# Loading chunks 6 and 7 in blocks and transposing them on VectorE in a fused retention and MLP kernel

## The chip, the cores and the metric

The kernel runs on one core of a Trainium2 chip. The metric is device time in microseconds (us) of one execution; lower is better. Each kernel is run several times, and the median stands for it.

TensorE does the matmuls and writes to PSUM, VectorE and ScalarE do elementwise work and copies out of PSUM, GpSimd does a few small things, and SyncE issues the transfers between memory and the core's SBUF.

## The reference

Two stages follow each other. The first is a retention layer with a decaying state, for 4 batches, 8 heads, 768 positions and a head size of 64. The second is an MLP with a gated activation over the 3072 rows of 512 values that the first gives.

```python
# q, k, v: (B=4, H=8, S=768, D=64), float32
gamma = 1.0 - 2.0 ** (-5.0 - np.arange(H))
state = 0
for t in range(S):
    state = gamma * state + einsum('bhd,bhe->bhde', k[:, :, t], v[:, :, t])
    y[:, :, t] = D ** -0.5 * einsum('bhd,bhde->bhe', q[:, :, t], state)

x = y.transpose(0, 2, 1, 3).reshape(3072, 512)
h = x @ w_in                       # (3072, 512) @ (512, 2048)
sp = softplus(h)
out = (h * erf(sp)) @ w_out        # (3072, 2048) @ (2048, 512)
```

The weights come as float64.

## The kernel before

The positions are cut into 24 chunks of 128 (6 for each batch), and chunk j goes through these steps: `K_` scales k and q by powers of the decay, `T` transposes k and q so that the head dimension lies on the partitions, `S_` multiplies k and q to scores, `M` masks them, `O_` makes the output and the new state, `A` adds to the state.

The MLP works on groups g, each of a quarter of the hidden units. Groups 0 to 3 are the plain groups: they handle the first 512 rows with ordinary matmuls (`hidden`, then the activation `gate`, then the second layer `project` of the group before). From group 4 (G0) on, each group handles 256 rows and computes its matrix products by seven products of half-size matrices with sums formed ahead (`hidden_part(g, p)` and `project_part(g, p)`, p from 1 to 7). During the plain groups VectorE also converts the float64 weights to float32, piece by piece.

Chunks from NB on are loaded differently: k a second time and q in 32x32 blocks, so placed that VectorE's transpose of single blocks gives the whole transposed chunk. Before the change NB is 8.

```python
    JPC = TCH // C                      # 4
    NB = 2 * JPC

    def load_blocks(to, src):
        for s, d in itertools.product(range(2), range(2)):
            part = slice((2 * s + d) * 32, (2 * s + d + 1) * 32)
            for u in range(HP):         # HP = 4
                nc.sync.dma_start(      # 16 transfers of 16 KB
                    to[part, u * C : (u + 1) * C].rearrange("p (a d) -> p a d", d=32),
                    src[2 * u + s, :, d * 32 : (d + 1) * 32].rearrange("(a p) d -> p a d", p=32),
                )

    def load(j):
        # ...
        else:
            KQ[j] = loads.tile([P, 2, H, D], F32, name="kq")      # 3 buffers
            V[j] = loads.tile([P, H, D], F32, name="v")           # 3 buffers
        now = slice(c * C, (c + 1) * C)
        if j >= NB:
            KB[j] = loads.tile([P, HP * C], F32, name="kb", bufs=2)
            nc.sync.dma_start(KQ[j][:, 0], k[b, :, now, :].rearrange("h p d -> p h d"))
            load_blocks(KQ[j][:, 1].rearrange("p h d -> p (h d)"), q[b, :, now, :])
            load_blocks(KB[j], k[b, :, now, :])
        for i, src in enumerate((k, q) if j < NB else ()):
            # ... one transfer of 256 KB each
        # ...
        nc.sync.dma_start(V[j], v[b, :, now, :].rearrange("h p d -> p h d"))

    def ret_scale(j):                                             # K_
        # ...
        if j >= NB:
            nc.vector.tensor_tensor(                              # L390
                KQ[j][:, 0], KQ[j][:, 0],
                kq_s[:, j % NC, 0, :, None].to_broadcast([P, H, D]), op=ALU.mult,
            )
            for i, x in enumerate((KB[j], KQ[j][:, 1].rearrange("p h d -> p (h d)"))):
                # ...
                by = kq_b[:, j % NC, i, :, :, None].to_broadcast([P, HP, 4, 32])
                nc.vector.tensor_tensor(x, x, by, op=ALU.mult)    # L397
            return
        by = kq_s[:, j % NC, :, :, None].to_broadcast([P, 2, H, D])
        nc.vector.tensor_tensor(KQ[j], KQ[j], by, op=ALU.mult)    # L400
        pace(-1.1)

    def ret_transpose(j):                                         # T
        if j >= NB:
            for name, store, x in (("k", KT, KB[j]), ("q", QT, ...)):
                store[j] = ret.tile([P, HP, C], F32, name=name + "T")
                nc.vector.transpose(store[j].rearrange("p u t -> p (u t)"), x)   # L410
            return
        for i, (name, store) in enumerate((("k", KT), ("q", QT))):
            p = ret_psum()
            for u in range(HP):
                nc.tensor.transpose(p[:, u, :], ..., ident)       # L415
            store[j] = ret.tile([P, HP, C], F32, name=name + "T")
            nc.scalar.copy(store[j], p)                           # L421
        pace(1)
```

The plain groups call their steps from a list, `after`, with one entry per `hidden(g, u)`: steps that run at once, and steps that are put into `waiting` and run in the middle of the next `hidden` or `project`. The steps of the second layer of group g - 1 stand at the end of group g.

```python
    for g in range(G0):
        for u in range(FG):
            if g and u == (2 if g == 1 else 0):
                waiting.append((gated, g - 1))
            hidden(g, u)
            run(after[g][u][0])
            waiting.extend(after[g][u][1])
        gate(g)
        if g:
            for tt in range(TT):
                project(g - 1, tt)
                if g == 1 and tt == 1:
                    waiting.append((K_, 5))
```

The first group after them, g = 4, for chunk j = 6:

```python
        hidden_part(g, 1)
        hidden_part(g, 2)
        if first:
            gated(g - 1)
        # ...
        if first:
            T(j)
        hidden_part(g, 6)
        if first:
            S_(j)
            M(j)
            K_(j + 1)
            block_scales()
        for _ in range(2):
            next(last_steps, None)
        # ...
        hidden_part(g, 5)
        if first:
            T(j + 1)
        hidden_part(g, 7)
        # ...
        if first:
            project(g - 1, 0)
        # ...
        hidden_part(g, 4)
        hidden_part(g, 3)
```

In `hidden_part`, products 1, 6, 7 and 4 use one PSUM bank and products 2, 5 and 3 the other. After product 2 VectorE adds its bank to h (L732), and product 5 then begins that bank anew. The products are L719, the plain first layer L648, the plain second layer `project` L662, and `project_part` L791.

Of the kernel before, what the change touches and what calls it, by code (L numbers as in the profile page):

```python
# [45 lines left out]
def kernel(  # L46
# [21 lines left out]
    JPC = TCH // C  # L68
# [15 lines left out]

    KQ, V, KB = {}, {}, {}

    NB = 2 * JPC

    def load_blocks(to, src):

# [4 lines that stand above are left out]
                nc.sync.dma_start(  # L95
# [5 lines that stand above are left out]
        b, c = divmod(j, NC)  # L101
        if j == JPC - 1:

            x = act.tile([P, N], F32, name="e", bufs=1)
            KQ[j] = x[:, : 2 * d_model].rearrange("p (i h d) -> p i h d", i=2, h=H)
            V[j] = x[:, 2 * d_model : 3 * d_model].rearrange("p (h d) -> p h d", h=H)
        else:
            KQ[j] = loads.tile([P, 2, H, D], F32, name="kq")
            V[j] = loads.tile([P, H, D], F32, name="v")
# [8 lines that stand above are left out]
            queue = nc.scalar if i and 0 < j < 3 else nc.sync  # L118
            queue.dma_start(KQ[j][:, i], src[b, :, now, :].rearrange("h p d -> p h d"))  # L119
        if j == JPC - 1:  # L120
            load_piece(0)
        nc.sync.dma_start(V[j], v[b, :, now, :].rearrange("h p d -> p h d"))
# [36 lines left out]
    def load_piece(n):  # L159
        which, i = pieces[n]  # L160
        w = raws[place[n]]
        if which == "in":
            for r in range(2):
                nc.sync.dma_start(
                    w[r * D : (r + 1) * D].rearrange("p (g f) -> p g f", g=n_k),
                    w_in[r * DH : (r + 1) * DH, i * 2 * P : (i + 1) * 2 * P].rearrange(
                        "(g p) f -> p g f", p=D
                    ),
                )
        else:  # L170
            for d in range(2):
                nc.sync.dma_start(
                    w.rearrange("p (d f c) -> p d f c", d=2, f=2)[:, d],
                    w_out[i * 2 * P : (i + 1) * 2 * P, d * DH : (d + 1) * DH].rearrange(
                        "(f p) c -> p f c", p=P
                    ),
                )
# [175 lines left out]
    def block_scales():  # L353
        nc.vector.reciprocal(by_b[:, 0], by_b[:, 1])
        nc.vector.reciprocal(kq_b[:, 0, 1], kq_b[:, 0, 0])
        nc.vector.tensor_scalar(kq_b[:, 0, 1], kq_b[:, 0, 1], unscale, None, op0=ALU.mult)
        for c in range(1, NC):
            nc.gpsimd.tensor_tensor(
                kq_b[:, c], kq_b[:, c - 1], by_b[:, :, :, None].to_broadcast([P, 2, HP, 4]),
                op=ALU.mult,  # L360
            )
# [16 lines left out]
    def ret_psum(pool=None):  # L378

        pool = pool or (next(psum_turn) if early else ps_r)  # L380
        return pool.tile([P, HP, C], F32, name="hp" if pool is ps_h else "r")
# [3 lines left out]
    def ret_scale(j):  # L385
        if j >= NJ:
            return
        scaled.add(j)
        if j >= NB:
            nc.vector.tensor_tensor(  # L390
# [12 lines left out]
    def ret_transpose(j):  # L403
        assert j in scaled
        if j >= NB:
            for name, store, x in (
# [196 lines left out]
    def gate(g):  # L603


        name = "r" if g < 4 and g % 2 else "e"
        E[g] = act.tile([P, N], F32, name=name, bufs=1)
        nc.scalar.activation(E[g], HS[g], AF.Softplus)  # L608

        if g:  # L610
            gate_erf(g)
# [8 lines left out]
    waiting = []  # L620
# [9 lines left out]
    def run(steps):  # L630
        for f, *args in steps:
            f(*args)

    def gated(g):
        for a in range(2):
            half = slice(a * N // 2, (a + 1) * N // 2)
            nc.vector.tensor_tensor(E[g][:, half], HS[g][:, half], E[g][:, half], op=ALU.mult)  # L637
        pace(-2.2)


    def hidden(g, u):
        ft = g * FG + u
        if u == 0:
            HS[g] = act.tile([P, N], F32, name="h")
        need("in", ft)
        p = ps_h.tile([P, TCH], F32, name="hp")
        for kk in range(n_k):
            nc.tensor.matmul(  # L648
                p, w_in_of(ft, kk), XC[0][:, kk, :], start=(kk == 0), stop=(kk == n_k - 1)
            )  # L650
        nc.scalar.copy(HS[g][:, u * TCH : (u + 1) * TCH], p)
        done.add(("hidden", ft))

        pace_around(3.4 if g else 2.5)
# [27 lines left out]
    G0 = n_ft // FG  # L682
# [5 lines left out]
    def chunk_of(g):  # L688
        return TCH // SCH + (g - G0) // 2
# [116 lines left out]
    def put_part(m, step):  # L806
# [27 lines left out]
    K_, T, S_, M, O_, A = (  # L834
        ret_scale, ret_transpose, ret_scores, ret_mask, ret_out, ret_add
    )
# [6 lines left out]
    for j in range(JPC):  # L843
# [8 lines left out]
        else:  # L852
# [19 lines left out]
            ([(S_, 4)], [(M, 4)]),  # L872
        ],
        [
            ([(O_, 4), (load, 6)], [(A, 4)]),
            ([(T, 5), (load, 7)], []),
            ([(S_, 5)], [(M, 5)]),
            ([(O_, 5)], [(A, 5)]),
        ],
        [  # L880
            ([(load_block_scales,)], []),
            ([], [(x_sums, G0)]),
            ([(load, 8)], [(K_, 6)]),
            ([], []),
        ],
    ]
    for g in range(G0):
# [10 lines that stand above are left out]
                project(g - 1, tt)  # L898
                if g == 1 and tt == 1:
                    waiting.append((K_, 5))  # L900

    j = JPC + 2
    put = None
    for g in range(G0, NG):
        first = g == G0
        more = j < NJ
# [4 lines that stand above are left out]
        if put is not None:  # L913
            for step in range(3):
                put_part(put, step)
        if first:
            T(j)
        hidden_part(g, 6)
        if first:
            S_(j)  # L920
            M(j)
            K_(j + 1)
            block_scales()
        for _ in range(2):
            next(last_steps, None)
        if put is not None:
            put_part(put, 3)
            put = None
        if not first:
            g_sums(g - 1)  # L930
        hidden_part(g, 5)
        if first:
            T(j + 1)
        hidden_part(g, 7)
        for _ in range(2):
            next(last_steps, None)
# [3 lines that stand above are left out]
            project_part(g - 1, 1)  # L940
        hidden_part(g, 4)
        hidden_part(g, 3)


        if more and not first:
            sub_visit(j, g)
        elif more:
            O_(j)
            A(j)
            SC[j + 1] = [ret_psum(ps_h) for _ in range(2)]  # L950
            sub_scores(j + 1)
            sub_mask(j + 1)
        if g + 1 < NG and (g - G0) % 2:
            x_sums(g + 1)
        if more:
            if j + 2 < NJ:
                K_(j + 2)
                T(j + 2)
            if j + 3 < NJ:
                load(j + 3)  # L960
            j += 1
        if first:
            gate(g)
            for tt in range(1, TT):
                project(g - 1, tt)
            put_first()
        else:
            for p in (2, 4):
                project_part(g - 1, p)
            gate(g)  # L970
            for p in (5, 6, 7, 3):
                project_part(g - 1, p)
            if (g - G0) % 2 == 0:
                put = chunk_of(g - 1)
        if g == NG - 1:
            last_gated(g)
        else:
            gated(g)

    g, m = NG - 1, chunk_of(NG - 1)  # L980
# [55 lines left out]
```

## Time and profile before

| | |
|---|---|
| median of 3 runs | 689.3 us (689.06 to 690.34) |
| profiled run, span | 688.0 us |
| ScalarE busy | 257.6 us (37%) |
| transfers | 47.12 MB, mean 68 GB/s |
| issues of 16 KB blocks on SyncE | 256 for q and 256 for k, median 1.8 and 1.7 us from issue to landing |
| issues of 256 KB of v | 23, median 3.1 us from issue to landing |

The profile is one execution as the hardware profiler took it. Its page gives the busy time of each engine, the chain of work that ended last (followed back from the last instruction to whatever released it), the groups of instructions by source line, and the transfers. An engine's instructions can also be listed in order of time, with the idle time before them and the instruction that ended it. A line such as L719 is a line of the kernel. PE is TensorE's matmul, PEld its weight load, DVE is VectorE, ACT is ScalarE, POOL is GpSimd, SPq is SyncE's queue of transfers.

### The profile page before, as it was taken

What the parts mean: (1) busy time and instruction counts of PE and PEld (TensorE: products, weight loads), DVE (VectorE), ACT (ScalarE), POOL (GpSimd) and SP (SyncE); (2) the same over time, 40 slices, a digit from 0 to 9 for tenths busy, and PEclk for the clock granted to TensorE, in tenths of its full rate; (3) what the DMA queues carried; (4) which work ended last, traced back from release to release, by engine and by line L of the source; (5) the groups of instructions that cost most, each with busy time, mean ns of one, the idle gap of its engine ahead of it and who ended that gap; (6) DMA issues with size and microseconds to landing.
All of it is one profiled execution on the core that took longest, in us unless ns stands there. A gap on an engine that the chain in (4) does not pass through costs nothing.

```text
span 688.0 us, 14344 instructions
## 1 busy us (share of the span) xinstructions
PE 678.0 (99%) x6214; PEld 577.8 (84%) x6214; DVE 384.0 (56%) x591; ACT 257.6 (37%) x293; POOL 6.6 (1%) x21
## 2 busy tenths in 40 slices
PE   8899999999999999999999999999999999999997
PEld 8544444586999999999999999999999999999996
DVE  4799999264954643653564455454544554343324
ACT  3377362425234144144242342441441432433430
POOL 2000000010000000000000000000000000000000
PEclk9999999999999999999999999999999999999999
DMA  9999963102322321322222222322222200000000
GB/s 193 212 239 243 240 193 62 28 1 44 104 39 40 75 43 35 75 33 46 64 47 44 67 41 46 71 37 44 51 60 41 48 34 1 2 32 1 1 31 32
DMA packets 147216, 47.12 MB, mean 68 GB/s; under 512 B 135760, under 2 KB 136016, under 8 KB 147152
## 3 DMA queue, kind: packets, MB, share of 16 engines
q1 hardware_dynamic: 144640, 45.66, 30.4%
q8 instruction: 49, 0.80, 0.5%
q10 hardware_dynamic: 2512, 0.53, 0.5%
q14 instruction: 15, 0.12, 0.1%
HBM read 39.86 MB, written 6.29 MB: 67 GB/s over the span
## 4 chain that ended last, share of the span: by engine, by line
PE 86%; DVE 8%; issue 2%; SPq 1%; DMA 1%; ACT 0%; DVEq 0%
PE hp L719 36%; PE o L791 36%; PE o L662 6%; PE hp L648 2%; PE r L527 1%; PE hp L492 1%; DVE w_out_sb L215 1%; DVE w_out_sb L220 1%; DMA e<-in_q_dram 1%; SPq L119 1%; DVE w_out_sb L223 1%; PE o L563 1%; DVE w_in_sb L223 1%; DVE w_in_sb L229 1%; PE hp L542 1%
## 5 line engine op out<-in xcount | busy, mean ns | idle before, releaser
L719 PE MATMUL hp<-xs,w_in_sb 128*128 128x128 f32 x1280 | 149.8, 275 | 0.0
L719 PEld LDWEIGHTS hp<-xs,w_in_sb 128*128 128x128 f32 x1280 | 147.8, 192 | 1.6 <-issue 0.5
L791 PE MATMUL o<-w_out_sb,h 128*128 128x256 f32 x640 | 141.7, 379 | 0.0
L791 PEld LDWEIGHTS o<-w_out_sb,h 128*128 128x128 f32 x640 | 121.6, 190 | 16.5
L719 PE MATMUL hp<-xT,w_in_sb 128*128 128x128 f32 x960 | 113.7, 275 | 0.0
L719 PEld LDWEIGHTS hp<-xT,w_in_sb 128*128 128x128 f32 x960 | 111.9, 192 | 1.9 <-issue 1.0
L791 PE MATMUL o<-w_out_sb,e 128*128 128x256 f32 x480 | 112.1, 383 | 0.0
L637 DVE TENSOR_TENSOR e<-h,e 128x1024 f32<-128x1024 f32 x42 | 49.6, 1222 | 102.7 <-ACT e L618 102.7
L791 PEld LDWEIGHTS o<-w_out_sb,e 128*128 128x128 f32 x480 | 88.2, 190 | 11.6
L648 PE MATMUL hp<-xT,w_in_sb 128*128 128x512 f32 x128 | 56.6, 595 | 0.8 <-DVE w_in_sb L229 0.7
L744 DVE TENSOR_TENSOR h<-h,hp 128x512 f32<-128x512 f32 x20 | 13.8, 688 | 75.3 <-PE hp L719 75.3
L608 ACT ACT_TABLE_LOAD x24 | 30.8, 1283 | 61.1 <-issue 45.4
L648 PEld LDWEIGHTS hp<-xT,w_in_sb 128*128 128x128 f32 x128 | 23.8, 190 | 29.8 <-issue 27.3
L618 ACT ACTIVATE e<-e 128x2048 f32<-128x2048 f32 (+1 forms) x23 | 42.1, 1836 | 0.2
L608 ACT ACTIVATE e<-h 128x2048 f32<-128x2048 f32 x22 | 42.0, 1910 | 0.2
L732 DVE TENSOR_TENSOR h<-h,hp 128x512 f32<-128x512 f32 x20 | 13.8, 688 | 49.6 <-PE hp L719 49.6
L742 ACT COPY h<-hp 128x512 f32<-128x512 f32 x20 | 11.7, 586 | 60.2 <-PE hp L719 60.2
L737 ACT COPY h<-hp 128x512 f32<-128x512 f32 x20 | 11.7, 587 | 57.9 <-PE hp L719 57.9
L735 ACT COPY h<-hp 128x512 f32<-128x512 f32 x20 | 11.7, 586 | 55.3 <-PE hp L719 55.3
L618 ACT ACT_TABLE_LOAD x24 | 30.8, 1283 | 0.4
L581 ACT COPY xT<-r 128x256 f32<-128x256 f32 x32 | 10.4, 375 | 54.8 <-PE r L527 54.8
L730 ACT COPY h<-hp 128x512 f32<-128x512 f32 x20 | 11.8, 588 | 48.3 <-PE hp L719 48.3
(134 smaller groups left out, 674.1 us busy)
## 6 DMA issues: line engine op xcount, KB each, us to landing
w_out_sb<-in_moe_w_out_dram SPq DMA_DIRECT2D x14, 512.0 KB, 5.7
w_in_sb<-in_moe_w_in_dram SPq DMA_DIRECT2D x12, 512.0 KB, 12.0
kq<-in_k_dram SPq DMA_DIRECT2D x23, 256.0 KB, 3.5
v<-in_v_dram SPq DMA_DIRECT2D x23, 256.0 KB, 3.1
out_dram<-r SPq DMA_DIRECT2D x23, 256.0 KB, 3.3
kq<-in_q_dram SPq DMA_DIRECT2D x256, 16.0 KB, 1.8
kb<-in_k_dram SPq DMA_DIRECT2D x256, 16.0 KB, 1.7
w_out_sb<-in_moe_w_in_dram SPq DMA_DIRECT2D x4, 512.0 KB, 10.3
```

Source lines behind the costliest of these rows:

```text
L223: nc.vector.scalar_tensor_tensor(power, hi, 1 << 31, power, op0=ALU.bitwise_and, op1=ALU.bitwise_or)
L608: nc.scalar.activation(E[g], HS[g], AF.Softplus)
L618: nc.scalar.activation(E[g][:, half], E[g][:, half], AF.Erf)
L637: nc.vector.tensor_tensor(E[g][:, half], HS[g][:, half], E[g][:, half], op=ALU.mult)
L648: nc.tensor.matmul(p, w_in_of(ft, kk), XC[0][:, kk, :], start=(kk == 0), stop=(kk == n_k - 1))
L662: nc.tensor.matmul(O[0][tt].rearrange("p (d c) -> p d c", d=2), E[g][:, u * TCH + tt * P : u * TCH + (tt + 1) * P], w_out_of(ft), start=(f ...
L719: nc.tensor.matmul(bank[:, u, :], w_in_sb[:, s, IN[a], kk, u * P : (u + 1) * P], XS[m][b][:, kk, :], start=(p in (1, 2, 5) and u == 0 and ...
L730: nc.scalar.copy(h["11"], flat)
L732: nc.vector.tensor_tensor(h["11"], h["11"], flat, op=ALU.add)
L735: nc.scalar.copy(h["12"], flat)
L744: nc.vector.tensor_tensor(h["12"], h["12"], flat, op=ALU.add)
L791: nc.tensor.matmul(O[m][i][:, half, :], G[g][a][:, u * P : (u + 1) * P], w_out_sb[:, s, OUT[b], u, :], start=i not in started, stop=(s == ...
```

## The change

Chunks 6 and 7 are treated as the later chunks are: NB goes from 8 to 6, so k and q of them come in blocks too, and VectorE transposes them, in place of TensorE with copies by ScalarE. For that the scales of the blocks have to be there earlier (`load_block_scales` still stands in group 3, but `block_scales` moves there as well), and the scaling and transposing of both chunks is put among the second-layer steps of group 3, the `project(2, tt)`. Their loads move from group 2 to group 3, after the scales, and the load of chunk 8 goes behind them. The aim is to take 16 transposes out of TensorE's stream and to use time in which VectorE has nothing to do.

```diff
-    NB = 2 * JPC
+    NB = JPC + 2
@@ the steps after hidden(g, u), for g = 2 and 3
         [
-            ([(O_, 4), (load, 6)], [(A, 4)]),
-            ([(T, 5), (load, 7)], []),
+            ([(O_, 4)], [(A, 4)]),
+            ([(T, 5)], []),
             ([(S_, 5)], [(M, 5)]),
             ([(O_, 5)], [(A, 5)]),
         ],
         [
-            ([(load_block_scales,)], []),
+            ([(load_block_scales,), (load, 6)], []),
+            ([(load, 7)], []),
             ([], [(x_sums, G0)]),
-            ([(load, 8)], [(K_, 6)]),
-            ([], []),
+            ([], [(block_scales,)]),
         ],
@@ after project(g - 1, tt)
                 if g == 1 and tt == 1:
                     waiting.append((K_, 5))
+                elif g == G0 - 1 and tt in (0, 2):
+                    waiting.extend([(K_, JPC + 2 + tt // 2), (T, JPC + 2 + tt // 2)])
+                elif g == G0 - 1 and tt == 1:
+                    load(JPC + 4)
@@ in the groups from G0 on
-        if first:
-            T(j)
         hidden_part(g, 6)
         if first:
             S_(j)
             M(j)
-            K_(j + 1)
-            block_scales()
@@
         hidden_part(g, 5)
-        if first:
-            T(j + 1)
         hidden_part(g, 7)
```

## The prediction

> **What bounds the kernel now.** I read the page first: busy times and the shares of the chain that ended last.
>
> ```profile
> PE 678.0 (99%) x6214; PEld 577.8 (84%) x6214; DVE 384.0 (56%) x591; ACT 257.6 (37%) x293; POOL 6.6 (1%) x21
> ...
> PE 86%; DVE 8%; issue 2%; SPq 1%; DMA 1%; ACT 0%; DVEq 0%
> ```
>
> TensorE is busy for 678.0 of 688.0 us, and the chain is its own work for 86%. VectorE's 8% lies before 92 us, where the chain in order of time steps through the weight conversions; after that it is TensorE alone up to the end. So a microsecond taken from TensorE's stream after 92 us counts in full, and a microsecond of waiting put into it counts in full too. The total of VectorE, 56%, tells nothing here: what matters is when one of its instructions is late.
>
> Next, TensorE's instructions in order of time, where the first group after the plain ones begins (columns: start us, us, engine, line, operation, tiles; a matmul is two records).
>
> ```profile
> 138.60 1.04 PE L415 MATMUL r<-ident,kq 128*128 128x128 f32 x8
> 139.47 1.95 PE L719 MATMUL hp<-xs,w_in_sb 128*128 128x128 f32 x16
> 141.35 1.16 PE L428 MATMUL r<-qT,kT 64*128 64x128 f32 x16
> 142.44 2.05 PE L719 MATMUL hp<-xs,w_in_sb 128*128 128x128 f32 x16
> 145.06 1.06 PE L415 MATMUL r<-ident,kq 128*128 128x128 f32 x8 [0.57 <-issue]
> 145.96 1.95 PE L719 MATMUL hp<-xs,w_in_sb 128*128 128x128 f32 x16
> ```
>
> L415 is the transposes of chunks 6 and 7, between the products 2, 6, 5 and 7. The first takes 139.47 - 138.60 = 0.87 us of the stream. The second takes 145.96 - 145.06 = 0.90, and 0.57 us stand idle before it: they end when VectorE has scaled chunk 7 (L400, next but one fence). A product of 16 records takes 1.79 us of the stream (the chain in order of time), so from start to start the second costs 145.96 - 142.44 - 1.79 = 1.73 us.
>
> Then SyncE's issues, as chunk 8 is already loaded in blocks by this kernel (columns as above; the duration is the time the queue spent on them).
>
> ```profile
> 100.86 8.59 SPq L347 DMA_DIRECT2D kq_b<-decay_k_dram  x16
> 109.50 0.43 SPq L351 DMA_DIRECT2D by_b<-decay_s_dram  x1
> 110.03 0.38 SPq L113 DMA_DIRECT2D kq<-in_k_dram  x1
> 110.45 7.70 SPq L95 DMA_DIRECT2D kq<-in_q_dram  x16
> 118.20 7.54 SPq L95 DMA_DIRECT2D kb<-in_k_dram  x16
> 125.84 0.38 SPq L122 DMA_DIRECT2D v<-in_v_dram  x1
> ```
>
> One chunk in blocks is 34 issues and holds SyncE from 110.03 to 126.22, that is 16.2 us (0.47 us each); the issues stand back to back. The group of L95 in this window lands 1.7 us after issue in the median. The last piece of the weights is issued at 99.93, so nothing in blocks can start sooner in this order.
>
> Last, VectorE's instructions (same columns).
>
> ```profile
> 138.87 0.69 DVE L732 TENSOR_TENSOR h<-h,hp 128x512 f32<-128x512 f32 x1 [14.18 <-PE hp L719]
> ...
> 143.75 1.22 DVE L400 TENSOR_TENSOR kq<-kq,kq_s 128x1024 f32<-128x1024 f32 x1
> ...
> 158.46 0.68 DVE L397 TENSOR_TENSOR kb<-kb,kq_b 128x512 f32<-128x512 f32 x1
> 159.07 0.68 DVE L397 TENSOR_TENSOR kq<-kq,kq_b 128x512 f32<-128x512 f32 x1
> 159.67 0.70 DVE L410 STREAM_TRANSPOSE kT<-kb 128x512 f32<-128x512 f32 x1
> 160.30 0.67 DVE L410 STREAM_TRANSPOSE qT<-kq 128x512 f32<-128x512 f32 x1
> ```
>
> L732 adds product 2 to h; product 5 writes the same PSUM bank with start=True, so TensorE can't begin product 5 before L732 has read it. VectorE idles 14.18 us before L732: the change puts its new work there. From the kb scaling on, four instructions of a block chunk take 160.97 - 158.46 = 2.5 us.
>
> **What the Trainium skill says.** "VectorE: DVE Perf Modes", The three transpose paths: VectorE transposes only within 32x32 blocks, which is why q and k have to arrive cut in blocks; the trace has such a transpose of 128x512 at 0.70 us. "DMA: Bandwidth & Descriptors", Rules for kernel authors: under 64 KB one pays mostly overhead. That agrees: a 16 KB block takes 1.7 us to land and 0.47 us of SyncE, against 3.5 us to land and 0.38 us of SyncE for a whole 256 KB k. "TensorE: Matmul & The Clock Gate", Architectural detail: VectorE's queue is strict FIFO; the trace shows its instructions in program order only. The same page, Part 1: after at least one idle window of about 3.4 us TensorE falls to half clock, and it takes a busy window to come back. This trace has no such gap in mid-kernel (TensorE's longest wait is 1.5 us, at the start), but its first dummy matmuls show the two speeds:
>
> ```profile
> L374 PE MATMUL o<-ident x7: 421/421/421, 2.7 to 4.0; 128*128 128x128 f32 x7
> ...
> L374 PE MATMUL o<-ident x11: 275/275/384, 5.7 to 6.9; 128*128 128x128 f32 x11
> ```
>
> Seven records in a microsecond become eleven or so somewhat before 6 us: about 4 us at half pace. (The granted clock stands at 1.00 throughout and does not show this.)
>
> **The change part by part.** Removed from TensorE: 2 x 4 transposes and the gap before the second, 0.87 + 1.73 = 2.6 us from start to start, all on the path. Removed from ScalarE: 4 copies of 0.59 us, off the path (ScalarE idles 3.68 us before one pair). Removed from VectorE: two L400 of 1.22 us. Added to VectorE: two chunks of three scalings and two transposes, 10 x 0.61 = 6.1 us, between its last weight step and L732. Two large loads leave SyncE between 77.4 and 90.1 us, where the DMA engines are full; but VectorE is 4.9 of 5 us busy there, with conversions that don't wait for data, so this brings nothing.
>
> Now the arrival of the blocks. In the changed program SyncE's order is: last weight piece (99.93, still released by VectorE's L223 that begins at 98.69), block scales (to 109.9), chunk 6, chunk 7, chunk 8. Chunk 6 takes the place that chunk 8 has now: 110.03 to 126.22, its last k block issued at 125.3 and landed at 127.0. VectorE, through with the conversions and scales near 124, does chunk 6 from 127.0 to 129.6. Chunk 7 follows at 126.3 and is 16.2 us later in every part: its last k block is issued at 141.6 and landed at 143.3.
>
> VectorE's order in the changed program is: scales, five instructions of chunk 6, five of chunk 7, and only then L732. So L732 can begin at 143.3 + 4 x 0.62 = 145.8 and ends at 146.5, against 139.5 now. On TensorE, product 2 still ends at 138.6; product 6 runs to 140.4, the scores of chunk 6 to 141.5; then product 5 waits for L732 until about 146.6: 5.1 us idle. Then product 5 to 148.4 and product 7 at once. Product 7 starts at 145.96 now, so the loss is 148.4 - 145.96 = 2.45 us. That is the wait of 5.1 us less the 2.6 us saved.
>
> Further on I find nothing to give it back or add to it. The gating of the last plain group ends at 149.0, before its projection at 150.2; L739 ends near 153.3, before product 3 needs it at 155.5. Chunk 8 is issued from 142.6 to 158.8 and landed near 160; VectorE comes to it at 157.86 + 2.5 = 160.4. Chunk 9 is issued by 176, needed at about 187. In the later groups SyncE spends 16 to 18 us of every 26.9 on a chunk, so it catches up.
>
> The wait of 5.1 us is longer than 3.4 us. If the clock is watched in free-running windows of that length, a whole idle one lies in it with a chance of (5.1 - 3.4) / 3.4 = 0.5. Half pace for about 4 us costs 2 us: +1.0 us on average. This rests on the page and the two lines above; no run here shows it in mid-kernel.
>
> Sum: 689.3 + 2.5 + 1.0 = 692.8 us; with a small weight for the first rival I put down 692.6 us.
>
> **The rivals.** First, the change works as meant: chunk 7 is there before L732 is due, and the 2.6 us are saved: 686.7. For it: VectorE has 14.18 us free just there, more than the 6.1 us added. Against it: not VectorE's time but SyncE's decides; 34 issues after 34 issues after 17 don't end before 142. It would need issues of 0.35 us. Second, the wait comes without the clock falling: 691.8. Third, with the fall and slower issues (later chunks show 8.9 us for 16 instead of 7.7): 1 us more of wait, 695. Fourth, chunk 8 is the late one, too, and holds up VectorE's gating: by the times above it has slack until the projections of the next group at 176, so nothing.
>
> **Range and chances.** The weights are about 0.12 for the first rival, 0.43 each for the wait without and with the fall of the clock. 688.5 to 695.5 us leaves out the first rival and the worst of the third. 2% is 13.8 us, far more than any of these: same 0.97; slower 0.02, should the wait repeat in later groups; faster 0.01.
>
> **What would show it.** Right, if the changed profile has no L415 after 100 us; chunk 6 issued near 110 and chunk 7 near 126 to 142; VectorE idle before the second L397 kb, released by a DMA near 143; and TensorE idle about 5 us before a product L719 with L732 as releaser. Matmuls of 421 ns instead of 275 after the wait would show the clock. Wrong, if SyncE reaches chunk 6 well before 110, or if product 5 starts near 141.5, or if there are waits in later groups that are not in this profile.

## The result, and the profile after

The changed kernel took 695.79 us (median of 4 runs, 694.55 to 697.23) against 689.47 us before (4 runs, 689.06 to 690.34): a ratio of 1.0091, 95% interval 1.0069 to 1.0113. It is slower by 0.9%, and the predicted 692.6 us and the range up to 695.5 us lie below it. The profiled run is the fastest of the four: its span is 692.8 us, against 688.0.

The first lines of the page of the changed kernel, busy times and chain:

```profile
PE 678.6 (98%) x6198; PEld 578.3 (83%) x6198; DVE 388.1 (56%) x599; ACT 255.5 (37%) x289; POOL 5.2 (1%) x21
...
PE 79%; DVE 8%; SPq 7%; DMA 3%; issue 2%; ACT 0%; DVEq 0%
```

TensorE has 16 matmul records less and is as busy as before, which already hints at slower matmuls. SyncE's queue, 1% of the chain before, is 7% of it now. Its list of waits on TensorE (us in total, times, longest) has a new first line:

```profile
PE hp L719 <- DVE h L732: 6.9, 1, 6.9
```

Two lines of the profile before, which the comparison below starts and ends with:

```profile
135.03 3.73 PE L719 MATMUL hp<-xT,w_in_sb 128*128 128x128 f32 x32
147.75 3.60 PE L662 MATMUL o<-w_out_sb,r 128*128 128x512 f32 x8
```

Now the same three views of the changed kernel, in order of time. First TensorE (the first line is products 1 and 2):

```profile
134.30 3.73 PE L719 MATMUL hp<-xT,w_in_sb 128*128 128x128 f32 x32
137.87 1.95 PE L719 MATMUL hp<-xs,w_in_sb 128*128 128x128 f32 x16
139.75 1.16 PE L428 MATMUL r<-qT,kT 64*128 64x128 f32 x16
147.82 5.34 PE L719 MATMUL hp<-xs,w_in_sb 128*128 128x128 f32 x32 [6.91 <-DVE h L732]
152.99 3.60 PE L662 MATMUL o<-w_out_sb,r 128*128 128x512 f32 x8
```

The transposes L415 of chunks 6 and 7 are gone. Product 5 stands behind 6.91 us of idle time, and products 5 and 7 together take 152.99 - 147.82 = 5.17 us up to L662, where two products take 3.58 at full clock. Their records last 421 ns in the median here, against 275 before: the sign that the prediction named for a fallen clock. Then SyncE:

```profile
109.36 0.39 SPq L113 DMA_DIRECT2D kq<-in_k_dram  x1
109.79 7.69 SPq L95 DMA_DIRECT2D kq<-in_q_dram  x16
117.53 7.54 SPq L95 DMA_DIRECT2D kb<-in_k_dram  x16
...
125.64 0.53 SPq L113 DMA_DIRECT2D kq<-in_k_dram  x1
126.22 8.00 SPq L95 DMA_DIRECT2D kq<-in_q_dram  x16
134.26 8.86 SPq L95 DMA_DIRECT2D kb<-in_k_dram  x16
143.16 0.43 SPq L122 DMA_DIRECT2D v<-in_v_dram  x1
```

Chunk 6 takes the place of chunk 8 before, and chunk 7 follows at once, but needs 8.00 + 8.86 us for its blocks, not 7.69 + 7.54. And VectorE:

```profile
129.61 0.69 DVE L390 TENSOR_TENSOR kq<-kq,kq_s 128x512 f32<-128x512 f32 x1 [0.50 <-DMA kq<-in_k_dram]
144.69 0.69 DVE L397 TENSOR_TENSOR kb<-kb,kq_b 128x512 f32<-128x512 f32 x1 [14.39 <-DMA kb<-in_k_dram]
145.29 0.68 DVE L397 TENSOR_TENSOR kq<-kq,kq_b 128x512 f32<-128x512 f32 x1
145.90 0.70 DVE L410 STREAM_TRANSPOSE kT<-kb 128x512 f32<-128x512 f32 x1
146.52 0.67 DVE L410 STREAM_TRANSPOSE qT<-kq 128x512 f32<-128x512 f32 x1
147.12 0.65 DVE L732 TENSOR_TENSOR h<-h,hp 128x512 f32<-128x512 f32 x1
```

VectorE stands for 14.39 us at the scaling of chunk 7's k blocks, until the last of them lands, and L732 runs only behind its four instructions. In stretches of 2 us (busy time of each engine, then the granted TensorE clock, the share of the transfer engines and GB/s):

```profile
142.00:144.00 2.00, 0.00 (x0) 0.00 (x0) 0.00 (x0) 0.00 (x0) 0.00 (x0) 1.00 0.23 34
144.00:146.00 2.00, 0.00 (x0) 0.00 (x0) 1.31 (x3) 0.00 (x0) 0.00 (x0) 0.54 0.81 183
148.00:150.00 2.00, 2.00 (x10) 2.00 (x11) 2.00 (x3) 0.00 (x0) 0.00 (x0) 0.50 0.21 33
150.00:152.00 2.00, 2.00 (x16) 2.00 (x16) 2.00 (x4) 0.00 (x0) 0.00 (x0) 0.75 0.21 33
```

The clock falls to half in the wait and stays there into products 5 and 7: the trace's record of the clock has it at half from 144.16 to 150.99 us.

### The profile page after: what moved, and what is told of

Read it like the earlier page. It is cut to its first block, busy times and chain, and to the rows that moved or that the text cites. A ratio compares the mean times of both kernels' runs of the same rounds, so it can differ in the third digit from the quotient of the medians.

```text
span 692.8 us, 14388 instructions
## 1 busy us (share of the span) xinstructions
PE 678.6 (98%) x6198; PEld 578.3 (83%) x6198; DVE 388.1 (56%) x599; ACT 255.5 (37%) x289; POOL 5.2 (1%) x21
## 4 chain that ended last, share of the span: by engine, by line
PE 79%; DVE 8%; SPq 7%; DMA 3%; issue 2%; ACT 0%; DVEq 0%
PE hp L719 36%; PE o L791 35%; SPq L95 4%; PE o L662 2%; DMA w_out_sb<-in_moe_w_out_dram 2%; PE r L527 1%; PE hp L492 1%; DVE w_out_sb L215 1%; DMA e<-in_q_dram 1%; PE o L563 1%; DVE w_in_sb L229 1%; DVE w_out_sb L220 1%; SPq L119 1%; DVE w_in_sb L223 1%; DVE w_out_sb L223 1%
## 5 line engine op out<-in xcount | busy, mean ns | idle before, releaser
L719 PEld LDWEIGHTS hp<-xs,w_in_sb 128*128 128x128 f32 x1280 | 149.3, 194 | 8.6 <-DVE h L732 7.1
L732 DVE TENSOR_TENSOR h<-h,hp 128x512 f32<-128x512 f32 x20 | 13.7, 686 | 35.8 <-PE hp L719 35.8
```

Source lines behind the costliest of these rows:

```text
L719: nc.tensor.matmul(bank[:, u, :], w_in_sb[:, s, IN[a], kk, u * P : (u + 1) * P], XS[m][b][:, kk, :], start=(p in (1, 2, 5) and u == 0 and ...
L732: nc.vector.tensor_tensor(h["11"], h["11"], flat, op=ALU.add)
```

## The experiments

The theory: chunk 7 arrives late, because SyncE issues its small blocks one after the other; on VectorE its work stands ahead of L732, so TensorE waits; and the wait lowers TensorE's clock. The rivals: the added work on VectorE is itself the cause; block chunks cost something wherever they stand; the clock is no part of it.

One measure serves all profiles: the time from the start of product 1 of group 4 to the start of the first projection L662 after product 7. It leaves out the first part of the kernel, whose length differs from run to run in all kernels (product 1 starts between 133.8 and 137.0 us in these profiles). Without waits, transposes and added work it is 10.22 us.

| kernel | median us | ratio to before (95%) | product 1 to L662, us | wait before product 5, us |
|---|---|---|---|---|
| before | 690.2 | | 12.72 | 0 |
| changed, first four runs | 695.79 | 1.0091 (1.0069 to 1.0113) | 18.69 | 6.91 |
| changed, beside the later runs | 696.87 | 1.009 (1.0076 to 1.0105) | 19.64 | 7.06 |
| only chunk 6 in blocks | 688.62 | 0.9979 (0.9971 to 0.9986) | 11.92 | 0 |
| chunk 7 later on VectorE | 687.22 | 0.9954 (0.9941 to 0.9966) | 10.22 | 0 |
| chunk 7 in whole transfers | 687.07 | 0.9956 (0.9941 to 0.9971) | 10.22 | 0 |
| scores five times | 696.26 | 1.0085 (1.0065 to 1.0104) | 18.60 | 3.12 |
| scores seven times | 693.8 | 1.0053 (1.004 to 1.0066) | 17.68 | 2.03 |
| 16 more issues | 702.02 | 1.0171 (1.0155 to 1.0187) | 27.45 | 14.52 |
| scales early, from GpSimd | 688.85 | 0.9976 (0.9967 to 0.9985) | 10.22 | 0 |

The median of before is that of its runs beside the experiments (690.23 beside four of them, 690.2 beside the others); the ratio of the first four runs is to 689.47.

### Only chunk 6 in blocks

```diff
-    NB = JPC + 2
+    BLOCKS = {JPC + 2, *range(2 * JPC, NJ)}     # and "j in BLOCKS" for "j >= NB"
@@
-                elif g == G0 - 1 and tt in (0, 2):
-                    waiting.extend([(K_, JPC + 2 + tt // 2), (T, JPC + 2 + tt // 2)])
+                elif g == G0 - 1 and tt == 0:
+                    waiting.extend([(K_, JPC + 2), (T, JPC + 2)])
@@ group 4: chunk 7 as before the change
             M(j)
+            K_(j + 1)
@@
         hidden_part(g, 5)
+        if first:
+            T(j + 1)
```

> Theory (chunk 7's blocks arrive too late and stand ahead of L732 on VectorE): with chunk 6 alone in blocks nothing on VectorE waits past 130 us, so no wait before product 5; TensorE saves the first transposes, 0.87 us: 688.6 us. Rival (the work or the small transfers of a block chunk cost something wherever they stand): half of the loss remains with half of the chunks, about 692 to 693 us.

It took 688.62 us, and there is no wait before product 5. Chunk 6 is no part of the loss: its half of the change brings what the sum said (0.8 us from product 1 to L662, 12.72 to 11.92). The medians differ by 1.6 us; where the other 0.8 come from was not tried. In the profiled run, one of the longer ones (690.29 us), the clock also falls once, far ahead of this place; the last section comes back to it.

### Chunk 7 later on VectorE

```diff
-                elif g == G0 - 1 and tt in (0, 2):
-                    waiting.extend([(K_, JPC + 2 + tt // 2), (T, JPC + 2 + tt // 2)])
+                elif g == G0 - 1 and tt == 0:
+                    waiting.extend([(K_, JPC + 2), (T, JPC + 2)])
@@ group 4
         hidden_part(g, 7)
+        if first:
+            K_(j + 1)
+            T(j + 1)
```

> Chunk 7 is still loaded in blocks at the same time, but VectorE scales and transposes it only after L739. Theory: L732 runs at once, no wait on TensorE, no fall of the clock, both transposes saved (2.6 us): 686.9 us. Rival (the late arrival costs wherever it is waited for, since the scores of chunk 7 or L744 come next): a wait moves to L744 or the scores, 690 us or more.

It took 687.22 us, faster than before and than the changed kernel. VectorE of this kernel, in order of time (its line numbers are one higher; L733 is L732, L740 is L739, L398 is the scaling L397):

```profile
139.27 0.69 DVE L733 TENSOR_TENSOR h<-h,hp 128x512 f32<-128x512 f32 x1 [8.88 <-PE hp L720]
...
146.47 0.69 DVE L740 TENSOR_TENSOR h<-h,hp 128x512 f32<-128x512 f32 x1 [0.65 <-ACT h L738]
147.07 0.68 DVE L391 TENSOR_TENSOR kq<-kq,kq_s 128x512 f32<-128x512 f32 x1
147.67 0.69 DVE L398 TENSOR_TENSOR kb<-kb,kq_b 128x512 f32<-128x512 f32 x1
```

The transfers are as late as before this edit: the last v of chunk 7 is issued at 143.86. But L733 runs at 139.27, as soon as product 2 is through, and by 147.67, when VectorE comes to the k blocks, they are there: no wait at all. TensorE goes through without a gap:

```profile
135.43 3.73 PE L720 MATMUL hp<-xT,w_in_sb 128*128 128x128 f32 x32
...
141.97 3.84 PE L720 MATMUL hp<-xs,w_in_sb 128*128 128x128 f32 x32
145.65 3.60 PE L663 MATMUL o<-w_out_sb,r 128*128 128x512 f32 x8
```

The place in VectorE's order is enough to turn the loss into the gain.

### Chunk 7 in whole transfers

```diff
-            load_blocks(KQ[j][:, 1].rearrange("p h d -> p (h d)"), q[b, :, now, :])
-            load_blocks(KB[j], k[b, :, now, :])
+            if j == JPC + 3:
+                nc.sync.dma_start(KQ[j][:, 1], q[b, :, now, :].rearrange("h p d -> p h d"))
+                nc.sync.dma_start(
+                    KB[j].rearrange("p (h d) -> p h d", h=H), k[b, :, now, :].rearrange("h p d -> p h d"))
+            else:
+                ...                                # as above
```

Chunk 7 is not cut in blocks here, so the output computed from it is not the reference's; all instructions of VectorE and TensorE stay.

> Chunk 7 comes in four whole transfers of 256 KB, not cut in blocks, so what is computed from it is not the reference; VectorE's and TensorE's instructions are those of the changed kernel. Theory (SyncE's issues make it late): chunk 7 is there near 131 us, VectorE is through with it by 134, no wait: 686.9 us. Rival (VectorE's added work ahead of L732 is the cause): still a wait at product 5, 691 us or more.

It took 687.07 us. SyncE, then VectorE of this kernel (L403 is the scaling L397, L738 is L732):

```profile
126.32 0.53 SPq L113 DMA_DIRECT2D kq<-in_k_dram  x1
126.89 0.89 SPq L115 DMA_DIRECT2D kq<-in_q_dram  x1
127.82 0.88 SPq L116 DMA_DIRECT2D kb<-in_k_dram  x1
```

```profile
132.75 0.69 DVE L403 TENSOR_TENSOR kb<-kb,kq_b 128x512 f32<-128x512 f32 x1 [1.79 <-DMA kb<-in_k_dram]
...
138.75 0.69 DVE L738 TENSOR_TENSOR h<-h,hp 128x512 f32<-128x512 f32 x1 [3.49 <-PE hp L725]
```

The same work stands ahead of L738, and yet VectorE idles 3.49 us before it. So VectorE's work by itself is not the cause. What differs is that q and the second k come in two transfers, not in 32 small ones; that it is the number of issues which counts is shown by the run with 16 more issues below.

### Scales early, from GpSimd

```diff
-                nc.sync.dma_start(kq_b[part, 0, 0, u], ...)
+                nc.gpsimd.dma_start(kq_b[part, 0, 0, u], ...)
-        nc.sync.dma_start(by_b[:, 1], decay_s)
+        nc.gpsimd.dma_start(by_b[:, 1], decay_s)
@@
-            ([(load_block_scales,), (load, 6)], []),
+            ([(load, 6)], []),
@@ at the start
     other_scales()
+    load_block_scales()
```

> The 17 transfers of the block scales go out at the start from GpSimd's queue, so SyncE begins chunk 6 at about 100.9 and chunk 7 at 117; the order on VectorE is the changed kernel's. Theory: the last block of chunk 7 is there at about 135.5, VectorE is through by 138.2, before L732 is due at 138.6, no wait: 687 us. If the issues stretch as in the changed kernel (1.3 us), a wait of 0 to 1 us, 687.5. Rival (VectorE's order alone decides): wait and time as in the changed kernel.

It took 688.85 us. The wait is gone in the changed kernel's own order. SyncE issued chunk 7 from 121.17 to 137.96, and VectorE, which had waited 9.12 us for it, had the last k block at 138.83 (the theory said 135.5); TensorE was later, too, and reached product 5 at 143.49, after L732, which ended at 141.91. The margin is thin, and in part luck: with product 1 at 135.66, as in the changed kernel beside it, product 5 would have been due at 142.20, by these figures. Product 1 starts at 136.95 us here, later than in any other profile, and by the profiles that is where the 1.6 us against the two kernels above went. A wait of 1.5 us for chunk 3's v stands among TensorE's early waits, where the changed kernel has none; whether the 17 early transfers cause it wasn't tried by itself.

### 16 more issues

```diff
-            ([(load, 7)], []),
+            ([(more_issues,), (load, 7)], []),    # 16 transfers of 0.5 KB to an unused tile
```

> 16 more transfers of 0.5 KB to an unused tile are issued just before chunk 7. Theory (SyncE's issues set the time at which chunk 7 is there): its last block comes 16 x 0.47 = 7.6 us later, and so does product 5; TensorE's wait grows from 6.9 to about 14.5 us and the whole from 695.8 to about 703.5 us. Rival (the bytes or the landing set it, or something else hides behind the wait): less than 3 us more.

It took 702.02 us; TensorE of this kernel:

```profile
133.81 3.73 PE L730 MATMUL hp<-xT,w_in_sb 128*128 128x128 f32 x32
...
154.94 6.49 PE L730 MATMUL hp<-xs,w_in_sb 128*128 128x128 f32 x32 [14.52 <-DVE h L743]
161.26 3.60 PE L673 MATMUL o<-w_out_sb,r 128*128 128x512 f32 x8
```

16 issues of 8 KB together lengthen the wait by 14.52 - 7.06 = 7.5 us, at 0.47 us each: SyncE's issue time goes into the wait one to one. The medians rose by 702.02 - 696.87 = 5.2 us and not by the expected 7.7. In the profiles, product 1 to L662 grew by 27.45 - 19.64 = 7.8 us, but product 1 started 1.85 us earlier than in the changed kernel beside it (133.81 against 135.66); the two profiled runs differ by 702.79 - 696.87 = 5.9 us. All four runs were below the expected 703.5 (701.01 to 702.79); why the first part is shorter in this kernel was not tried.

### Scores five and seven times

```diff
             S_(j)
+            for _ in range(4):                     # 6 in the second run
+                for hp in range(HP):
+                    for s in range(2):
+                        nc.tensor.matmul(SC[j][s][:, hp, :], ...)   # the same scores again
             M(j)
```

> The scores of chunk 6 are computed five times, so TensorE works for 4.4 us of the wait. Theory that the clock falls in the wait and costs 1.6 us in the profiled run and more in others: products 5 and 7 take 3.6 us together and not 5.2, the granted clock is 1.000, the time falls from 695.8 by 1.6 to 2.5 us to about 693.5, and the runs lie closer together. Rival (the slow matmuls have another cause, or the wait alone is the loss): 695.8 or more.

This one missed: 696.26 us, as the changed kernel. The repeats took 3.7 us, not 4.4, and 3.12 us of idle time were left. TensorE:

```profile
141.40 3.74 PE L926 MATMUL r<-qT,kT 64*128 64x128 f32 x64
148.26 5.47 PE L719 MATMUL hp<-xs,w_in_sb 128*128 128x128 f32 x32 [3.12 <-DVE h L732]
```

Products 5 and 7 are still slow; the clock now falls at 148.80, just after product 5 has begun, and rises at 152.21. With six repeats the gap is shorter:

> As the run with the scores five times, but seven times: TensorE then idles only 1.3 us before product 5. Theory (a stretch of 3.4 us that is mostly idle is what lowers the clock; four repeats left 3.1 us and the clock still fell): the granted clock stays at 1.00, products 5 and 7 take 3.6 us together, and the time is 1.6 us or more below the changed kernel's, about 693.5 to 694. Rival (the clock falls whatever fills the wait, or its fall costs nothing): as the changed kernel.

```profile
142.06 5.53 PE L926 MATMUL r<-qT,kT 64*128 64x128 f32 x96
149.62 3.84 PE L719 MATMUL hp<-xs,w_in_sb 128*128 128x128 f32 x32 [2.03 <-DVE h L732]
```

With 2.03 us of idle time left, the clock stays at 1.00, products 5 and 7 take 153.29 - 149.62 = 3.67 us up to L662, where they take 5.97 in the changed kernel beside it, and the kernel takes 693.8 us, 3.1 us less than the changed kernel beside it (intervals of the ratios apart: 1.004 to 1.0066 and 1.0076 to 1.0105). The fall of the clock is a loss of its own, on top of the wait. The runs with five scores show the same among themselves: 693.74 us at a mean clock of 1.000, 695.12 twice at 0.998, and 697.4 to 698.03 at 0.994 to 0.995. So do the kernels without this wait: of the 22 runs with only chunk 6 in blocks, the five with a mean clock of 0.997 or 0.998 took 690.09 to 690.80 us, the others 687.89 to 689.19.

### The changed kernel again

> The changed kernel again, beside the other three on this chip: 695.8 us and a wait of 6.9 us. The fall of the clock in every run, two or three stretches of 3.4 us long, would put the runs some 1.7 us apart.

It took 696.87 us, with a wait of 7.06 us and products 5 and 7 in 155.30 - 149.33 = 5.97 us. All nine runs of the changed kernel have a mean clock of 0.992 or 0.995, where no run of before beside the experiments is under 0.998, so the clock fell in each of them. The three runs at 0.992 took 696.95 to 697.23 us, the six at 0.995 694.55 to 696.87.

## Why the prediction was wrong

The chain of causes was right at every link; two terms of the sum were too small: the time until chunk 7's blocks are there, and with it the wait, and the chance that the clock falls.

- **TensorE's saving.** Predicted 2.6 us. From product 1 to L662 it is 12.72 - 10.22 = 2.50 us in the three kernels that have both chunks in VectorE's transposes and no wait. Right. (The "2 x 4 transposes" are 2 x 8 in the code, of one record each: the page counts 16 records less. The sum rests on their measured time and isn't touched.)
- **VectorE's order.** Chunk 7's five instructions stand ahead of L732, and TensorE waits for L732 at product 5. Shown by moving them (687.22 us) and by making their data early (687.07 us).
- **The time at which chunk 7 is there.** This step failed: "Chunk 7 follows at 126.3 and is 16.2 us later in every part". Chunk 7's last k block was issued 142.69 - 125.64 = 17.05 us after its first transfer, where 125.3 - 110.03 = 15.3 us were taken over from chunk 8 before, and it landed 1.9 us later, not 1.7. These 1.75 us are nearly the whole of the 6.91 - 5.1 = 1.8 us by which the wait came out too short. Two issues are stretched: the first q block, 0.88 us, and one k block at 139.48, 1.74 us, in place of 0.43. In the second profile of the changed kernel they are 0.98 and 1.70. The long one falls together with a fetch of instructions in the transfer queues in each of these profiles (at 139.42 and 140.96 us); that this is its cause was not tried. In the profile of before a fetch stands at 140.09 us, where SyncE issues nothing, so chunk 8 there could not show it. The profile of before showed the size: its later chunks took 8.2 to 9.6 us for 16 q blocks. I used that for a rival of 1 us and took the shortest case for the estimate. The wait became 6.91 and 7.06 us, and not 5.1.
- **The clock.** The fall was predicted with a chance of 0.5 and a cost of 2 us, 1.0 on average. It fell in all nine runs, and cost 5.17 - 3.58 = 1.59 us in the first profile and 5.97 - 3.58 = 2.39 in the second. What failed is "a whole idle one lies in it with a chance of (5.1 - 3.4) / 3.4": in a wait of 6.9 us or more a whole stretch of 3.4 us always fits, and the run with five scores shows that a stretch need not be wholly idle.
- **The sum by stage.** Measured in the first profile: 6.91 + 1.59 - 2.50 = 6.0 us, and from product 1 to L662 it is 18.69 - 12.72 = 5.97. Predicted: 5.1 + 1.0 - 2.6 = 3.5 us. That is the error of the prediction; the medians differ by 6.3 us.
- **Elsewhere nothing.** Right: from L662 to the end it is 692.8 - 152.99 = 539.8 us, against 688.0 - 147.75 = 540.3 before, and no later wait is new. That the two plain loads gone from 77 to 90 us bring nothing was right as well: what moved product 1 from 135.03 to 134.30 seems to stand at 20 us, where both kernels are alike (the wait for the state L595 is 1.4 us before and 0.4 us after).
- **The range.** The third rival had both errors together, the fall and slower issues, and put them at 695 us, with 1 us for the issues where 1.75 were measured; the range left out "the worst of the third", and that is what came. The 692.6 does not follow from the weights given with it, either: 0.12, 0.43 and 0.43 on 686.7, 691.8 and 693.8 us give 692.1. The change is less than 2%, as the chances had it.

## What to carry to other kernels

Work put into an engine's idle time runs in that engine's order, so ask of it when its data are there, and put it behind whatever somebody else waits for; here moving five instructions further back in one queue turned a loss of 0.9% into a gain of 0.5%. Transfers cut into small pieces were timed here by the queue that issues them: count the issues ahead of the last one, and take the time of one issue from several chunks rather than from the quickest. And a wait of TensorE can cost more than its length: in the two profiles of the changed kernel the fallen clock added 1.6 and 2.4 us to waits of some 7 us.

## What was unexpected of the hardware

The clock is granted in stretches of 3.41 us: in the traces' records it was low for 6.83 us in both profiles of the changed kernel (144.16 to 150.99 and 147.34 to 154.17), 3.41 us with five scores (148.80 to 152.21) and 17.07 us with 16 more issues (143.46 to 160.53), that is two, two, one and five such stretches; and the times at full clock ahead of these falls, 136.53, 139.95, 143.36 and 136.53 us, are 40, 41, 42 and 40 of them. The Trainium skill, "TensorE: Matmul & The Clock Gate", Part 1, has the length and the free-running window, and these runs agree. The runs differ from the page where it asks for at least one idle window: an idle time of 3.12 us was enough with five scores, less than one window, and with only chunk 6 in blocks a single one of 1.88 us was (us in total, times, longest; then stretches of 1 us as above):

```profile
PE r L415 <- DVE state L595: 1.9, 1, 1.9
```

```profile
19.00:20.00 1.00, 0.00 (x0) 0.00 (x0) 0.80 (x1) 0.00 (x0) 0.00 (x0) 1.00 1.07 205
...
22.00:23.00 1.00, 1.00 (x17) 0.73 (x16) 0.00 (x0) 0.74 (x2) 0.00 (x0) 0.50 1.13 200
```

There the clock is low from 21.53 to 24.94 us, one stretch. With seven scores, 2.03 us of idle time did not lower it; 1.79 of them lie in one stretch and the rest in the one before, while the 1.88 us lie within one stretch. So the length of a wait alone does not decide, and where the limit lies was not tried. A clock that was low stayed low over a stretch with 1.98 us of idle time in the second profile of the changed kernel. How long the low clock lasts into the work after the wait depends on where the stretches lie; it goes with the spread of the runs, 693.74 to 698.03 us with five scores.
